# Decode attention on one core: two heads per pass on 64 partitions each, V in 64 KB runs, one loop over all pairs

## Chip, cores, metric

One NeuronCore of one Trainium2 chip; its neighbours are idle. The metric is device time in microseconds for one execution.

## The reference

One new token for 2 batches attends over a key/value cache of 32 heads x 16384 keys x 128 (bf16); beside it runs a small MLP mixer on the same input, and a gate mixes the two. Cut to the part that matters:

```python
B, Sq, D = 2, 1, 1024
H, Sk, Dh = 32, 16384, 128
q = (x @ wq).reshape(B, Sq, H, Dh).transpose(0, 2, 1, 3)
scores = einsum("bhqd,bhkd->bhqk", q, k_cache) * Dh ** -0.5
o = einsum("bhqk,bhkd->bhqd", softmax(scores), v_cache)
a = o.transpose(0, 2, 1, 3).reshape(B, Sq, H * Dh) @ wo
# b = mixer MLP on x (weights w2, w3, w4);  result: g * a + (1 - g) * b
```

K and V are 64 x 4 MB each (a head of one batch: 16384 x 128 x 2 bytes), 537 MB in all, and 33 MB of weights. Each byte is used once.

## The kernel before

It loops over the 64 (head, batch) pairs g. A ring of four slots of 32 KB per partition (4 MB) takes all loads in queue order; a load is issued when a slot is released. A head is spread over all 128 partitions, 128 keys each.

```python
NRS = 4                                   # ring slots, 32 KB per partition each
def kv_src(T, g):
    h, b = g // 2, g % 2
    return T[b, h].rearrange("(p j) d -> p (j d)", p=P)      # 128 partitions x 32 KB
def q_k(g): queue_load(("k", g), [... e.dma_start(ring[:, idx, :], kv_src(A_k, g))])
def q_v(g): queue_load(("v", g), [... e.dma_start(ring[:, idx, :], kv_src(A_v, g))])

def do_T(g, u):      # K, 32x32 blocks transposed in place, an eighth of a slot at a time
    ap = ring[:, slot_of[("k", g)], u * JU * Dh:(u + 1) * JU * Dh].bitcast(F32)
    ev_T[(g, u)] = pl.add("dve", lambda e: e.transpose(ap, ap), waits=(arrived(("k", g)),), sig=True)
# do_S(g, u): 4 score matmuls of 512 columns; after u == NU - 1: release(("k", g), ev)
# softmax chain: do_rmax do_mt do_m do_mb do_negm do_exp do_PT (max, exp, transposed P), do_l do_rc (1/sum)
# do_PV(g): 32 matmuls of 512 columns; then release(("v", g), ev).  do_ext, do_OT: output column

for g in range(G + 2):                    # software pipeline over g, g-1, g-2
    if g < G: do_Z(g)
    for u in range(NU):
        if g < G: do_T(g, u); do_S(g, u)
        if u == 1 and 0 <= g - 2 < G: do_ext(g - 2); do_OT(g - 2)
    if g < G: do_rmax(g); ...; do_exp(g); do_PT(g)
    if 0 <= g - 1 < G: do_PV(g - 1); do_accc(g - 1)
    if g < G: do_l(g); do_rc(g)
GL, GE = 4, G - 2                         # heads 4..61 run in a hardware loop (two per turn); the rest is written out
# ... (cuts: weights, MLP, gate, output projection)
```

The load order is K0, K1, V0, K2, V1, ...; the last loads are pieces of wo, and the last piece's matmuls end the program.

Of the kernel before, what the change touches and what calls it, by code (L numbers as in the profile page):

```python
# [23 lines left out]
class _Plan:  # L24
# [18 lines left out]
    def add(self, eng, fn, waits=(), sig=False):  # L43
        ev = None
        if sig:
            self.cnt[eng] += 1
            ev = _Ev(self.esem[eng], self.cnt[eng])
        self.ops[eng].append((self._merge(waits), fn, ev, 1))
        return ev

    def dma(self, eng, fn, sem, waits=()):
        key = sem.num
        self.dcnt[key] = self.dcnt.get(key, 0) + 16
        ev = _Ev(sem, self.dcnt[key])
        self.ops[eng].append((self._merge(waits), fn, ev, 16))
        return ev
# [10 lines left out]
    @staticmethod  # L67
    def _put(eng, op, waits, base=None, delta=None):
        _, fn, ev, inc = op
        for w in waits:  # L70
            eng.wait_ge(w.sem, w.val if base is None else base * delta[w.sem.num] + w.val)  # L71
        ins = fn(eng)
        if ev is not None:
            ins.then_inc(ev.sem, inc)
# [44 lines left out]
def build_kernel(nc, A_x, A_k, A_v, A_wq, A_wo, B_w1, B_w2, B_w3, B_w4, gate_w, out, dbg=None):  # L119
# [9 lines left out]
    NU = 8  # L129
    JU = J // NU  # L130
    NBP = 4
    G = B * H
    NBD = D // P
# [22 lines left out]
    with ExitStack() as st:  # L156
# [10 lines left out]
        dsel = sb("dsel", [P, 4], BF16)  # L167
# [9 lines left out]
        Z = sb("Z", [P, 2, NBP, ZW], BF16)  # L177
        P_sb = sb("P_sb", [P, 2, NCOL], BF16)
        PT_sb = sb("PT_sb", [P, 2, NCOL], BF16)
        acc_sb = sb("acc_sb", [P, 512], BF16)  # L180
        rowsum = sb("rowsum", [P, 2], F32)
        rmax_bf = sb("rmax_bf", [P, 2], BF16)
        m_sb = sb("m_sb", [1, 2], BF16)
        negm = sb("negm", [P, 2], F32)
        recip = sb("recip", [P, 2], F32)
        OT_sb = sb("OT_sb", [P, G], BF16)
        OTp = sb("OTp", [P, 2], BF16)
        rA = sb("rA", [P, 2], F32)
# [48 lines left out]
        pconst(lambda e: e.memset(ones_f[:, :], 1.0))  # L237
        pconst(lambda e: e.memset(neg_half[:, :], -0.5))
# [8 lines left out]
        e0 = pconst(lambda e: e.memset(dsel[:, :], 0.0))  # L247
        for cg in range(4):
            pconst(aff(dsel[32 * cg:32 * cg + 32, :], -8 * (cg // 2), [[-2, 4]], 1), (e0,))
        e0 = pconst(lambda e: e.memset(rowm[:, :, :], 0.0))  # L250
        ev_rowm = pconst(aff(rowm[:, :, :], 0, [[-32, 4], [-2, NU]], 1), (e0,))
        pconst(lambda e: e.memset(Z[:, :, :, :], 0.0))
# [13 lines left out]
        slot_of = {}  # L266
        slot_free = {i: () for i in range(NRS)}
# [7 lines left out]
        def queue_load(key, fns):  # L275
            dma_q.append((key, fns))

        def pump():
            while dma_q and slot_free:
                key, fns = dma_q.pop(0)  # L280
                idx = next(iter(slot_free))
                waits = slot_free.pop(idx)
                slot_of[key] = idx
                for k, fn in enumerate(fns):
                    dsem = s_ring[idx] if len(fns) == 1 else s_tail[k]
                    dma_done[key] = dma_done[key, k] = pl.dma("sp", (lambda e, fn=fn, idx=idx: fn(e, idx)), dsem,
                                                              waits=waits if k == 0 else ())

        def release(key, ev):
            idx = slot_of[key]  # L290
            assert idx not in slot_free
            slot_free[idx] = tuple(ev) if isinstance(ev, (tuple, list)) else (ev,)
            pump()
# [42 lines left out]

        def q_load(key):
            queue_load(key, wloads[key])

        def kv_src(T, g):  # L340
            h, b = g // 2, g % 2
            return T[b, h].rearrange("(p j) d -> p (j d)", p=P)

        def q_k(g):
            queue_load(("k", g), [lambda e, idx: e.dma_start(ring[:, idx, :], kv_src(A_k, g))])

        def q_v(g):
            queue_load(("v", g), [lambda e, idx: e.dma_start(ring[:, idx, :], kv_src(A_v, g))])
# [37 lines left out]
        def st_gate():  # L386
# [10 lines left out]
                              waits=(e4,), sig=True)  # L397
            e5 = pl.add("dve", lambda e: e.tensor_tensor(gm[:, :], gT[:, 2:4], m2[:, :], op=ALU.mult),
# [153 lines left out]
        q_k(0)  # L552
        for g in range(1, G + 2):
            if g < G:
                q_k(g)
            if g - 1 < G:
                q_v(g - 1)
        for pi in range(len(wo_parts)):
            q_load(("wo", pi))
# [51 lines left out]
        def S_ps(par):  # L611
            return banks[3 + par]

# [3 lines left out]
        l_ps = banks[0][:, 128:129]  # L617
        oT_ps = banks[7][:, 0:1]

        ev_T = {}; ev_Z = {}; ev_S = {}; ev_P = {}; ev_PT = {}; ev_PV = {}; ev_OT = {}; ev_OTc = {}; ev_rmax = {}; ev_m = {}; ev_mt = {}  # L620
        ev_mb = {}; ev_negm = {}; ev_l = {}; ev_rc = {}; ev_accc = {}; ev_ext = {}

        def do_Z(g):
            pg = g % 2
            ev_Z[g] = pl.add("pool", lambda e: e.tensor_tensor(
                Z[:, pg, :, ZO:ZO + P].rearrange("p t (i c) -> p t i c", c=32)[:, :, :, 0],
                q4_f[:, :, g:g + 1].broadcast_to([P, NBP, 4]), mask4[:, :].unsqueeze(1).broadcast_to([P, NBP, 4]), op=ALU.mult),
                waits=(ev_q4, ev_const, ev_S.get(g - 2)), sig=True)

        def do_T(g, u):  # L630
            ap = ring[:, slot_of[("k", g)], u * JU * Dh:(u + 1) * JU * Dh].bitcast(F32)
            ev_T[(g, u)] = pl.add("dve", lambda e: e.transpose(ap, ap), waits=(arrived(("k", g)),), sig=True)  # L632

        def do_S(g, u):
            pg = g % 2
            kv = ring[:, slot_of[("k", g)], u * JU * Dh:(u + 1) * JU * Dh].rearrange("p (j b k t) -> p j b k t", j=JU, b=2, k=32)
            for bp in range(NBP):
                last = bp == NBP - 1
                w = ()
                if bp == 0:  # L640
                    w = (ev_T[(g, u)],)
                    if u == 0:
                        w += (ev_Z[g], ev_P.get(g - 2)) + (pro_ev if g < 2 else ())
                ev = pl.add("pe", lambda e, bp=bp: e.matmul(  # L644
                    S_ps(pg)[:, 0:NCOL], lhsT=Z[:, pg, bp, ZO - 2 * u:ZO - 2 * u + P], rhs=kv[:, :, bp // 2, :, bp % 2],
                    start=(u == 0 and bp == 0), stop=(u == NU - 1 and last), skip_group_check=True),
                    waits=w, sig=(last and u == NU - 1))
            if u == NU - 1:
                ev_S[g] = ev
                release(("k", g), ev)  # L650

        def do_PV(g):
            pg = g % 2
            vv = ring[:, slot_of[("v", g)], :].rearrange("p (u j d) -> p u j d", u=NU, j=JU)
            w = (ev_PT[g], arrived(("v", g)), ev_accc.get(g - 1))
            for jj in range(JU):
                for hf in range(2):
                    cg = 2 * hf + jj % 2
                    last = jj == JU - 1 and hf == 1
                    ev = pl.add("pe", lambda e, jj=jj, hf=hf, cg=cg: e.matmul(  # L660
                        acc_ps[32 * cg:32 * cg + 32, 0:512], lhsT=PT_sb[:, pg, 32 * jj:32 * jj + 32], rhs=vv[:, 4 * hf:4 * hf + 4, jj, :],
                        start=(jj < 2), stop=(jj >= JU - 2), tile_position=(0, 32 * cg), skip_group_check=True), waits=w, sig=last)
                    w = ()
            ev_PV[g] = ev
            release(("v", g), ev)

        def do_rmax(g):
            pg = g % 2
            e1 = pl.add("dve", lambda e: e.tensor_reduce(rA[:, pg:pg + 1], S_ps(pg)[:, 0:NCOL], axis=AX.X, op=ALU.max),  # L669
                        waits=(ev_S[g],), sig=True)  # L670
            ev_rmax[g] = pl.add("dve", lambda e: e.tensor_scalar(rmax_bf[:, pg:pg + 1], rA[:, pg:pg + 1], cAB[:, 1:2], None, op0=ALU.add),  # L671
                                waits=(e1, ev_cab if g == 0 else None, ev_mt.get(g - 2)), sig=True)

        def do_mt(g):
            pg = g % 2
            ev_mt[g] = pl.add("pe", lambda e: e.transpose(mt_ps, rmax_bf[:, pg:pg + 1], ident[:, :]),  # L676
                              waits=(ev_rmax[g], ev_m.get(g - 1), ev_ident if g == 0 else None) + (pro_ev if g == 0 else ()), sig=True)

        def do_m(g):
            pg = g % 2  # L680
            ev_m[g] = pl.add("dve", lambda e: e.tensor_reduce(m_sb[0:1, pg:pg + 1], mt_ps, axis=AX.X, op=ALU.max),  # L681
                             waits=(ev_mt[g], ev_mb.get(g - 2)), sig=True)

        def do_mb(g):
            pg = g % 2
# [171 lines left out]
```

## Time and profile before

| | before |
|---|---|
| time | 1333.47 us (1333.34 to 1333.58, 3 runs) |
| HBM traffic | 570.4 MB |
| rate over the span / from 300 to 1200 us | 429 / 432 GB/s |
| time for two heads (K and V), late in the run | 38.86 us |

The last row is the mean time between two loads into the same ring slot, by their last completions in the trace; in this kernel a slot comes round every fourth 4 MB load.

Abbreviations in the profile: PE is the matrix engine and PEld its weight loads, DVE the vector engine, ACT the scalar engine, POOL GpSimd, SP the engine that issues the loads; q1, q8 are DMA queues; L644 is line 644 of the kernel. "Granted clock" is the share of its full clock that PE was given, "DMA share" the share of time in which the 16 DMA engines were busy.

The main queue's packets fill 99.7% of the span on all 16 engines, while no compute engine is over 65%. A K load is issued 25.2 us and a V load 31.2 us before it lands, though 4 MB take 9.7 us: loads queue behind one another, and the DMA engines never run out of work.

The same by windows, 300 to 1200 us (each engine's busy time, then granted clock, DMA share, GB/s):

```profile
core 0: us, PE busy (x) PEld busy (x) DVE busy (x) ACT busy (x) POOL busy (x), PEclk, DMA share, GB/s
300.00:1200.00 900.00, 600.75 (x3327) 230.22 (x3326) 545.23 (x695) 63.28 (x138) 18.77 (x94) 0.81 1.00 432
```

The DMA share is 1.00 here: in this stretch the time is bytes over rate, and only the rate or the bytes can change it.

### The profile page before, as it was taken

How to read it: one execution, taken by the hardware profiler on the slowest of the kernel's cores; microseconds unless marked ns; L12 is line 12 of the kernel's file. 1: busy time of each engine (PE TensorE's matmuls, PEld its weight loads, DVE VectorE, ACT ScalarE, POOL GpSimd, SP SyncE). 2: the span in 40 equal slices, each digit the busy share in tenths (PEclk: the TensorE clock that was granted, in tenths of full speed). 3: DMA queues.
4: the chain of work that ended last, by engine and by line, in shares of the span. 5: the costliest groups of instructions: out<-in, count | busy, mean ns of one | idle time of the engine just before them, and what ended most of it. 6: DMA issues, size and time to landing. Idle time of an engine off the chain costs nothing.

```text
span 1331.4 us, 14124 instructions
## 1 busy us (share of the span) xinstructions
PE 860.8 (65%) x5466; PEld 343.8 (26%) x5466; DVE 762.6 (57%) x1000; ACT 89.7 (7%) x195; POOL 32.9 (2%) x161
## 2 busy tenths in 40 slices
PE   3466666667666666666766676676667666666765
PEld 3322222222222222222222222222222222222222
DVE  1076566566656656665665666566566656656661
ACT  0000000000000000000000000000000000000000
POOL 1000000000000000000000000000000000000000
PEclk9978887787888778778878878977787788778787
DMA  9999999999999999999999999999999999999998
GB/s 401 431 425 433 433 428 435 428 434 432 432 431 428 437 429 432 432 431 434 428 432 432 432 432 429 433 432 432 431 430 435 430 431 433 432 431 430 433 431 344
DMA packets 21652, 570.65 MB, mean 429 GB/s; under 512 B 2291, under 2 KB 2307, under 8 KB 2694
## 3 DMA queue, kind: packets, MB, share of 16 engines
q1 hardware_dynamic: 21608, 570.44, 99.7%
q8 instruction: 11, 0.18, 0.1%
q14 instruction: 3, 0.02, 0.0%
q10 hardware_dynamic: 30, 0.01, 0.0%
HBM read 570.44 MB, written 0.00 MB: 428 GB/s over the span
## 4 chain that ended last, share of the span: by engine, by line
DMA 64%; PE 25%; DVE 8%; issue 2%; SPq 0%; DVEq 0%; ACT 0%; POOL 0%
DMA ring<-in_A_k_cache_dram 61%; PE ps L644 23%; DVE ring L632 7%; DMA ring<-in_A_wo_dram 2%; DMA ring<-in_A_wq_dram 2%; DVE OTp L727 1%; PE ps L461 0%; PE ps L590 0%; SPq L312 0%; PE ps L711 0%; PE ps L490 0%; PE ps L383 0%; DVEq L71 0%; ACT P_sb L697 0%; POOL mv L424 0%
## 5 line engine op out<-in xcount | busy, mean ns | idle before, releaser
L644 PE MATMUL ps<-ring,Z 128*128 128x512 bf16 x2048 | 655.6, 480 | 326.0 <-DVE ring L632 320.2
L632 DVE STREAM_TRANSPOSE ring<-ring 128x1024 f32<-128x1024 f32 x512 | 591.0, 1212 | 117.3 <-DMA ring<-in_A_k_cache_dram 117.3
L644 PEld LDWEIGHTS ps<-ring,Z 128*128 128x128 bf16 x2048 | 216.6, 114 | 692.5 <-issue 376.3
L660 PE MATMUL ps<-ring,PT_sb 128*32 128x512 bf16 x2048 | 123.7, 384 | 2.3 <-DMA ring<-in_A_v_cache_dram 2.3
L697 ACT ACTIVATE P_sb<-ps,negm 128x512 bf16<-128x512 f32 x64 | 44.0, 688 | 1118.9 <-DVE negm L691 1118.9
L727 DVE TENSOR_SCALAR OTp<-ps,recip,gT 128x1 bf16<-128x1 f32 x64 | 17.9, 280 | 159.9 <-PE ps L711 159.9
L669 DVE TENSOR_REDUCE rA<-ps 128x1 f32<-128x512 f32 x64 | 44.2, 691 | 100.4 <-PE ps L644 100.4
L703 DVE STREAM_TRANSPOSE PT_sb<-P_sb 128x512 bf16<-128x512 bf16 x64 | 45.5, 711 | 54.1 <-ACT P_sb L697 54.1
L660 PEld LDWEIGHTS ps<-ring,PT_sb 128*32 128x32 bf16 x2048 | 49.3, 97 | 45.8 <-issue 3.8
L676 PE MATMUL ps<-ident,rmax_bf 128*1 128x128 bf16 x64 | 13.9, 217 | 66.2 <-DVE rmax_bf L671 66.2
L706 ACT ACTIVATE acc_sb<-ps 128x512 bf16<-128x512 f32 x64 | 38.2, 597 | 53.9 <-PE ps L660 53.9
L730 POOL COPY OT_sb<-OTp 128x1 bf16<-128x1 bf16 x64 | 11.9, 186 | 1204.1 <-DVE OTp L727 1204.1
L676 PEld LDWEIGHTS ps<-ident,rmax_bf 128*1 128x1 bf16 x64 | 5.1, 79 | 97.8 <-DVE rmax_bf L671 97.8
L681 DVE TENSOR_REDUCE m_sb<-ps 1x1 bf16<-1x128 bf16 x64 | 18.0, 281 | 19.7 <-PE ps L676 19.7
L711 PEld LDWEIGHTS ps<-dsel,acc_sb 128*128 128x128 bf16 x256 | 20.4, 118 | 33.7 <-issue 30.0
L691 DVE TENSOR_SCALAR negm<-ps,cAB 128x1 f32<-128x1 f32 x64 | 17.7, 277 | 17.2 <-PE ps L686 17.2
L686 PE MATMUL ps<-m_sb,ones_bf 1*128 1x1 bf16 x64 | 11.0, 172 | 24.0 <-DVE m_sb L681 24.0
L718 PEld LDWEIGHTS ps<-rowsum,ones_f 128*128 128x128 f32 x128 | 19.2, 189 | 28.0 <-issue 26.8
L718 PE MATMUL ps<-rowsum,ones_f 128*128 128x1 f32 x128 | 24.7, 262 | 1.2 <-ACT P_sb L697 1.2
L723 DVE RECIPROCAL recip<-ps 128x1 f32<-128x1 f32 x64 | 10.7, 168 | 19.9 <-PE ps L718 19.9
L590 PE MATMUL ps<-xT_bf,ring 128*128 128x2 bf16 x256 | 7.1, 165 | 17.8 <-DMA ring<-in_A_wq_dram 17.8
L711 PE MATMUL ps<-dsel,acc_sb 128*128 128x1 bf16 x256 | 17.5, 172 | 1.1 <-ACT acc_sb L706 1.1
(91 smaller groups left out, 122.9 us busy)
## 6 DMA issues: line engine op xcount, KB each, us to landing
ring<-in_A_k_cache_dram SPq DMA_DIRECT2D x64, 4096.0 KB, 25.2
ring<-in_A_v_cache_dram SPq DMA_DIRECT2D x64, 4096.0 KB, 31.2
ring<-in_A_wq_dram SPq DMA_DIRECT2D x2, 4096.0 KB, 17.5
ring<-in_B_w_dram SPq DMA_DIRECT2D x2, 3584.0 KB, 32.4
ring<-in_B_w_dram SPq DMA_DIRECT2D x1, 4096.0 KB, 28.3
ring<-in_A_wo_dram SPq DMA_DIRECT2D x1, 4096.0 KB, 32.2
ring<-in_B_w_dram SPq DMA_DIRECT2D x1, 3072.0 KB, 29.0
ring<-in_A_wo_dram SPq DMA_DIRECT2D x3, 1024.0 KB, 21.3
```

The source lines that it names most:

```text
L632: ev_T[(g, u)] = pl.add("dve", lambda e: e.transpose(ap, ap), waits=(arrived(("k", g)),), sig=True)
L644: ev = pl.add("pe", lambda e, bp=bp: e.matmul(S_ps(pg)[:, 0:NCOL], lhsT=Z[:, pg, bp, ZO - 2 * u:ZO - 2 * u + P], rhs=kv[:, :, bp // 2, :, ...
L660: ev = pl.add("pe", lambda e, jj=jj, hf=hf, cg=cg: e.matmul(acc_ps[32 * cg:32 * cg + 32, 0:512], lhsT=PT_sb[:, pg, 32 * jj:32 * jj + 32], ...
L669: e1 = pl.add("dve", lambda e: e.tensor_reduce(rA[:, pg:pg + 1], S_ps(pg)[:, 0:NCOL], axis=AX.X, op=ALU.max), waits=(ev_S[g],), sig=True)
L676: ev_mt[g] = pl.add("pe", lambda e: e.transpose(mt_ps, rmax_bf[:, pg:pg + 1], ident[:, :]), waits=(ev_rmax[g], ev_m.get(g - 1), ev_ident i ...
L681: ev_m[g] = pl.add("dve", lambda e: e.tensor_reduce(m_sb[0:1, pg:pg + 1], mt_ps, axis=AX.X, op=ALU.max), waits=(ev_mt[g], ev_mb.get(g - 2) ...
L697: ev_P[g] = pl.add("act", lambda e: e.activation(P_sb[:, pg, :], S_ps(pg)[:, 0:NCOL], ACT.Exp, bias=negm[:, pg:pg + 1], scale=scale, accum ...
L703: ev_PT[g] = pl.add("dve", lambda e: e.transpose(PT_sb[:, pg, :], P_sb[:, pg, :]), waits=(ev_P[g], ev_PV.get(g - 2)), sig=True)
L706: ev_accc[g] = pl.add("act", lambda e: e.activation(acc_sb[:, :], acc_ps[:, 0:512], ACT.Copy), waits=(ev_PV[g], ev_ext.get(g - 1)), sig=True)
L711: ev = pl.add("pe", lambda e, w=w: e.matmul(oT_ps, lhsT=acc_sb[:, w * P:(w + 1) * P], rhs=dsel[:, w:w + 1], start=(w == 0), stop=(w == 3)) ...
L718: ev_l[g] = pl.add("pe", lambda e: e.matmul(l_ps, lhsT=ones_f[:, :], rhs=rowsum[:, pg:pg + 1], start=True, stop=True), waits=(ev_P[g], ev_ ...
L727: ev_OT[g] = pl.add("dve", lambda e: e.tensor_scalar(OTp[:, pg:pg + 1], oT_ps, recip[:, pg:pg + 1], gT[:, pg:pg + 1], op0=ALU.mult, op1=AL ...
```

## The change

Intent: fewer and longer DMA runs, fewer softmax chains, a program that is one loop. Two heads of a batch share a pass: 64 partitions each, 256 keys per partition, so a partition's row is 64 KB in K and in V. V comes as one 8 MB load with 64 KB runs into two adjacent slots; K comes as two halves of 32 KB per row, so that each half's slot is free early. One softmax chain serves the pair; transposes are twice as long. The three-stage pipeline over heads is gone: each pair runs scores, softmax, PV and output in order, and all 32 pairs are turns of one loop.

```diff
-    NU = 8
-    JU = J // NU
+    HP = 2
+    NU = 16
+    JU = HP * J // NU
+    UH = NU // HP
+    NPR = G // HP
...
-        def kv_src(T, g):
-            h, b = g // 2, g % 2
-            return T[b, h].rearrange("(p j) d -> p (j d)", p=P)
+        w_slots = [0, 1, 2, 3, 0, 1, 2]
+        k_slots = (3, 2)
+        def kv_src(T, n):
+            h, b = n // B * HP, n % B
+            return T[b, h:h + HP].rearrange("h (p j) d -> (h p) (j d)", p=P // HP)
+        def q_k(n):
+            for t in range(2):
+                queue_load(("k", n, t), [lambda e, idx, t=t: e.dma_start(ring[:, idx, :], kv_src(A_k, n)[:, t * SLOT:(t + 1) * SLOT])],
+                           (k_slots[t],))
+        def q_v(n):
+            queue_load(("v", n), [lambda e, idx: e.dma_start(ring[:, idx:idx + 2, :].rearrange("p s m -> p (s m)"), kv_src(A_v, n))],
+                       (0, 1))
...
+        TC = 2
+        def do_T(n, c):
+            key, o = ("k", n, c * TC // UH), c * TC % UH * JU * Dh
+            ap = ring[:, slot_of[key], o:o + TC * JU * Dh].bitcast(F32)
+            return pl.add("dve", lambda e: e.transpose(ap, ap), waits=(arrived(key),), sig=True)
...
-        for g in range(G + 2):
-            ... (as above)
+        for n in range(NPR):
+            ev_z = do_Z(n)
+            for c in range(NU // TC):
+                ev_t = do_T(n, c)
+                for t in range(TC):
+                    do_S(n, c * TC + t, ...)
+            ev_pt, ev_rc = do_softmax(n)
+            ev_OT = do_out(n, do_PV(n, ev_pt), ev_rc)
...
-        GL, GE = 4, G - 2
-            first = pl.mark[GL][name]
-            return first, pl.mark[GL + 2][name] - first, (GE - GL) // 2
+            first = pl.mark[0][name]
+            return first, pl.mark[1][name] - first, NPR
```

## The prediction

> **What bounds the kernel now.** The DMA engines. On the page the main DMA queue's packets fill 99.7% of the 16 engines' span. By windows, 300 to 1200 us moves 432 GB/s at DMA share 1.00, while PE is busy 601, DVE 545 and ACT 63 of those 900 us. The chain that ended last gives DMA 64%; its PE and DVE shares only lie between a K landing and the next K issue. By the issue list a K load lands 25.2 us after its issue, V 31.2, against about 9.7 us of transfer (4 MB at 432 GB/s): one or two whole loads always wait behind the one in flight. The Trainium skill ("DMA: Bandwidth & Descriptors", Where 436 GB/s comes from) gives a port ceiling of 435.2 GB/s; this trace is within 1% of it. 570 MB at that ceiling still take 1310 us, so over 2% faster (below 1307) is practically excluded.
>
> **What the change does.**
> - Bytes: unchanged.
> - V: 4096 descriptors of 64 KB instead of 8192 of 32 KB. Packet records before: 8 KB 0.312, 28 KB 1.062, 32 KB 1.218 us. A line through the first two leaves about 12 ns per packet that doesn't grow with size. 256 packets fewer per engine x 12 ns = 3 us, on the critical path, the only such item. If the run is cut in two below the program, zero.
> - 32 DMAs fewer: completion records of 9 ns x 32 per engine = 0.3 us.
> - K: the same 32 KB packets, now half of a 64 KB row. I expect 1.22 us still.
> - Off the path: one softmax chain per pair instead of two; transposes of 2048 instead of 1024 elements (1212 ns now, estimate for double 2.3 us: about 30 us of DVE in all). Score and V matmuls stay 2048 each. DVE and ACT fall; the time doesn't follow.
> - Lost: overlap. Each pair runs scores, softmax, PV, output strictly in order. From the first K half's landing at 0: scores done at 12 us (transposes 9.3, last 8 matmuls 2.4), slot free; second half lands at 9.7, free at 22; softmax to 27; V (8 MB) lands at 29, its slots free by 33 to 35. By then the queue holds K of the next pair until 48.6: V is issued some 14 us ahead of need, K some 17. No bubble.
> - Start: same weight order; the second K half waits for the last w4 matmuls (66.2 us) while the first is in flight until 73. Tail: unchanged, the last wo piece.
>
> **Predicted: 1330 us, range 1322 to 1338.** Chances: faster by over 2% 0.01, within 2% 0.95, slower 0.04.
>
> **What would show the steps right.** DMA share 1.00 in the middle at 433 to 434 GB/s; V packets of 65,536 B at about 2.42 us; K packets at 1.22 us; K issue to landing about 27 us, V about 35; DVE down by roughly 50 us, ACT roughly halved, PE about the same; the chain still led by DMA.
>
> **What would make it wrong.** (1) DMA share below 1 between pairs, a slot freed too late: each 1 us per pair costs 32 us. (2) K packets slowed by the 64 KB row pitch; the skill's row-pitch entry (same page, Latency and other measured facts) starts at 512 KiB, no run here shows 64 KB. (3) 64 KB runs cut in two: 1333. (4) The 16 engines ending differently in the tail (a load's sixteen completions are 3.2 us apart now): +-2 us.

(The 1310 us in it is an estimate from that page's ceiling; at the measured 432 GB/s the same bytes take 1320 us.)

## More of the kernel before

From the page of the kernel before: busy time of each engine, DMA queues (packets, MB, share of the 16 engines' span), the chain that ended last, the two largest groups (busy us, mean ns of one, then idle time and its releaser), and for the K and V loads the KB of each and the median us from issue to landing.

```profile
span 1331.4 us, 14124 instructions
...
PE 860.8 (65%) x5466; PEld 343.8 (26%) x5466; DVE 762.6 (57%) x1000; ACT 89.7 (7%) x195; POOL 32.9 (2%) x161
...
q1 hardware_dynamic: 21608, 570.44, 99.7%
q8 instruction: 11, 0.18, 0.1%
...
DMA 64%; PE 25%; DVE 8%; issue 2%; SPq 0%; DVEq 0%; ACT 0%; POOL 0%
...
L644 PE MATMUL ps<-ring,Z 128*128 128x512 bf16 x2048 | 655.6, 480 | 326.0 <-DVE ring L632 320.2
L632 DVE STREAM_TRANSPOSE ring<-ring 128x1024 f32<-128x1024 f32 x512 | 591.0, 1212 | 117.3 <-DMA ring<-in_A_k_cache_dram 117.3
...
ring<-in_A_k_cache_dram SPq DMA_DIRECT2D x64, 4096.0 KB, 25.2
ring<-in_A_v_cache_dram SPq DMA_DIRECT2D x64, 4096.0 KB, 31.2
```

## The result, and the profile after

| | before | after |
|---|---|---|
| time | 1333.40 us (1333.33 to 1333.58, 4 runs) | 1329.43 us (1329.39 to 1329.61, 4 runs) |
| two heads, late in the run | 38.86 us | 38.78 us |
| last load's sixteen completions, first to last | 3.19 us | 1.88 us |

The ratio is 0.997, 95% interval 0.9953 to 0.9988: small, and clear of noise. Ratios here are the mean time of one kernel's runs over that of the other's runs of the same rounds, so not quite the ratio of the medians in the table. Executions over 1.5% slower than the fastest of the same kernel are left out of the means.

The page after, the lines that answer to those of before:

```profile
span 1327.6 us, 12590 instructions
...
PE 803.9 (61%) x5306; PEld 327.0 (25%) x5306; DVE 659.3 (50%) x521; ACT 45.7 (3%) x99; POOL 20.1 (2%) x101
...
q1 hardware_dynamic: 17000, 570.43, 99.7%
q8 instruction: 8, 0.13, 0.0%
...
DMA 72%; DVE 16%; PE 6%; issue 6%; SPq 0%; ACT 0%
...
L664 PE MATMUL ps<-ring,Z 128*128 128x512 bf16 x2048 | 540.0, 418 | 217.8 <-DVE ring L657 217.3
L657 DVE STREAM_TRANSPOSE ring<-ring 128x2048 f32<-128x2048 f32 x256 | 569.0, 2280 | 108.6 <-DMA ring<-in_A_k_cache_dram 108.6
...
ring<-in_A_k_cache_dram SPq DMA_DIRECT2D x64, 4096.0 KB, 27.8
```

The V loads' line stands in the list of DMA issues of the kernel after:

```profile
ring<-in_A_v_cache_dram SPq DMA_DIRECT2D x32, 33.0
```

And its windows, 300 to 1200 us:

```profile
300.00:1200.00 900.00, 553.53 (x3233) 216.05 (x3225) 469.67 (x347) 32.21 (x70) 8.81 (x46) 0.79 1.00 433
```

DVE lost 103 us of busy time, ACT half of its own, PE 57 us, and the time fell by 4. The DMA queue is as full as before (99.7%, share 1.00); its rate went from 432 to 433 GB/s. K and V still land 28 and 33 us after their issue, so loads still queue. There are 4.6 thousand packets fewer, and 8 instruction packets in place of 11.

The packet records of the two traces, by size (count, mean us of one):

```
size       before            after
 28 KB      256  1.070        256  1.069
 32 KB    16640  1.218       8448  1.218
 64 KB        -              4096  2.422
```

So a 64 KB run is one packet of 65,536 bytes. A K packet still takes 1.218 us although it is now half of a 64 KB row.

Where do the 4.0 us come from? Time per two heads fell by 0.076 us, which is 2.4 us over 32 pairs. The rest, about 1.5 us, does not accumulate in the steady part. The trace has the completion of each of the 16 engines for each load, and shows it there: before, the spread from the first to the last engine was 1.81 us for the load that landed at 180.1 us and 3.09 us for the next, at 191.1, and it stayed near 3.2 to the end; after, it is 1.9 from 56 us to the end. The last load shows both parts: its first completion came at 1324.98 us before and at 1322.53 after, 2.45 us earlier; its last at 1328.17 and 1324.41, 3.76 us earlier. (The two profiled executions took 1333.23 and 1329.41 us, 3.82 apart, so what the medians show beyond 3.8 lies between executions.) A load counts as landed only when its last engine is done, so the slower of two equally busy kernels can be the one whose slowest engine is further behind. (The Trainium skill, "DMA: Bandwidth & Descriptors", Why a DMA increments its semaphore by 16 and not by 1, says that the engines finish independently and only the full count means that all data landed. This trace agrees: each load has sixteen completions, the last load's 3.19 us apart before and 1.88 after.)

What set one engine back at 180 us? These records lie there, in the kernel before (start us, queue, kind, bytes, duration):

```
180.58 q8 instruction       16384 B  1.086 us
181.65 q1 hardware_dynamic  32768 B  1.694 us      (1.218 usual)
```

An instruction fetch of 16 KB took a DMA engine for 1.09 us, and a data packet that starts at its end took 0.48 us more than usual: 1.56 us together. That both ran on the same engine is read from their times; the trace does not say which engine a packet ran on. It was the ninth fetch of that run. Other fetches show the same: in a_peel24 (below) each of the 27 fetches among the K and V loads has one such packet, 0.46 to 0.55 us longer than usual.

That leaves two theories for the gain, and a rival:

- **P, packets:** each long run saves the fixed cost of one packet. Worth 2.4 us.
- **F, fetches:** the one-loop program is shorter, needs fewer instruction fetches, and its slowest DMA engine is hit once in place of twice. Worth about 1.3 us.
- **C, compute or number of DMAs:** half the softmax chains, longer transposes, 32 loads fewer. By the trace worth nothing.

### The profile page after: what moved, and what is told of

The parts are those of the page before. It is cut to its first block, busy times and chain, and to the rows that moved or that the text cites. A ratio compares the mean times of both kernels' runs of the same rounds, so it can differ in the third digit from the quotient of the medians.

```text
span 1327.6 us, 12590 instructions
## 1 busy us (share of the span) xinstructions
PE 803.9 (61%) x5306; PEld 327.0 (25%) x5306; DVE 659.3 (50%) x521; ACT 45.7 (3%) x99; POOL 20.1 (2%) x101
## 3 DMA queue, kind: packets, MB, share of 16 engines
q1 hardware_dynamic: 17000, 570.43, 99.7%
## 4 chain that ended last, share of the span: by engine, by line
DMA 72%; DVE 16%; PE 6%; issue 6%; SPq 0%; ACT 0%
DMA ring<-in_A_k_cache_dram 66%; DVE ring L657 16%; PE ps L664 5%; DMA ring<-in_B_w_dram 2%; DMA ring<-in_A_wo_dram 2%; DMA ring<-in_A_wq_dram 2%; SPq L324 0%; PE ps L514 0%; PE ps L612 0%; PE ps L485 0%; PE ps L405 0%; DVE orow L756 0%; DVE q_f L624 0%; PE ps L734 0%; PE ps L621 0%
## 5 line engine op out<-in xcount | busy, mean ns | idle before, releaser
L664 PE MATMUL ps<-ring,Z 128*128 128x512 bf16 x2048 | 540.0, 418 | 217.8 <-DVE ring L657 217.3
L657 DVE STREAM_TRANSPOSE ring<-ring 128x2048 f32<-128x2048 f32 x256 | 569.0, 2280 | 108.6 <-DMA ring<-in_A_k_cache_dram 108.6
L700 PE MATMUL ps<-ring,PT_sb 128*32 128x512 bf16 x2048 | 183.4, 537 | 152.7 <-DMA ring<-in_A_v_cache_dram 152.7
L700 PEld LDWEIGHTS ps<-ring,PT_sb 128*32 128x32 bf16 x2048 | 67.6, 130 | 255.4 <-DMA ring<-in_A_v_cache_dram 155.4
L674 DVE TENSOR_REDUCE rA<-ps 128x1 f32<-128x512 f32 x32 | 22.1, 691 | 64.3 <-PE ps L664 64.3
L685 ACT ACTIVATE P_sb<-ps,negm 128x512 bf16<-128x512 f32 x32 | 22.0, 687 | 851.5 <-DVE negm L683 851.5
L689 PE MATMUL ps<-rowsum,hsel 128*128 128x1 f32 x128 | 23.8, 290 | 37.9 <-ACT P_sb L685 37.9
L687 DVE STREAM_TRANSPOSE PT_sb<-P_sb 128x512 bf16<-128x512 bf16 x32 | 22.8, 711 | 27.0 <-ACT P_sb L685 27.0
L709 ACT ACTIVATE acc_sb<-ps 128x512 bf16<-128x512 f32 x32 | 19.1, 597 | 363.4 <-PE ps L700 363.4
L689 PEld LDWEIGHTS ps<-rowsum,hsel 128*128 128x128 f32 x128 | 21.1, 234 | 40.7 <-ACT P_sb L685 40.7
## 6 DMA issues: line engine op xcount, KB each, us to landing
ring<-in_A_k_cache_dram SPq DMA_DIRECT2D x64, 4096.0 KB, 27.8
```

The lines of the kernel that those rows point to most:

```text
L657: return pl.add("dve", lambda e: e.transpose(ap, ap), waits=(arrived(key),), sig=True)
L664: ev = pl.add("pe", lambda e, bp=bp: e.matmul(S_ps[:, 0:NCOL], lhsT=Z[:, bp, ZO - 2 * u:ZO - 2 * u + P], rhs=kv[:, :, bp // 2, :, bp % 2], ...
L674: e1 = pl.add("dve", lambda e: e.tensor_reduce(rA[:, :], S_ps[:, 0:NCOL], axis=AX.X, op=ALU.max), waits=(ev_S[n],), sig=True)
L685: e7 = pl.add("act", lambda e: e.activation(P_sb[:, :], S_ps[:, 0:NCOL], ACT.Exp, bias=negm[:, 0:1], scale=scale, accum_out=rowsum[:, 0:1] ...
L687: e8 = pl.add("dve", lambda e: e.transpose(PT_sb[:, :], P_sb[:, :]), waits=(e7,), sig=True)
L689: e9 = pl.add("pe", lambda e, hp=hp: e.matmul(l_ps[:, hp:hp + 1], lhsT=hsel[:, hp, :], rhs=rowsum[:, 0:1], start=True, stop=True, skip_gro ...
```

## The experiments

Labels: a_ is the kernel after with one thing changed; c_ goes further. All gave correct results. "Pair" is the time of two heads in the steady part, "fetches" the q8 packets of the run, "spread" the time from the first to the last engine's completion of the last wo load. The experiments were run in two batches on two chips; the kernel before took 1333.50 and 1333.39 us in them, so times of different rows compare within some 0.1 us.

| run | time us | ratio to before (95%) | pair us | fetches | spread us |
|---|---|---|---|---|---|
| before | 1333.40 | | 38.856 | 11 | 3.19 |
| after | 1329.43 | 0.997 (0.9953 to 0.9988) | 38.780 | 8 | 1.88 |
| a_v32 | 1332.04 | 0.9989 (0.9975 to 1.0003) | 38.858 | 8 | 2.11 |
| a_peel8 | 1331.01 | 0.9982 (0.9968 to 0.9996) | 38.78, to 760 us | 16 | 3.63 |
| a_peel24 | 1335.45 | 1.0014 (1.0001 to 1.0028) | 38.79, between jumps | 34 | 8.10 |
| a_soft2 | 1329.46 | 0.9971 (0.9956 to 0.9986) | 38.777 | 8 | 1.64 |
| a_soft4 | 1468.9 | 1.1016 (1.0996 to 1.1037) | 43.2 | 8 | 0.64 |
| a_kone | 1425.55 | 1.069 (1.0671 to 1.071) | 41.55 | 8 | 1.63 |
| c_k64 | 1328.35 | 0.9962 (0.9949 to 0.9976) | 38.702 | 9 | 3.04 |
| c_k64s | 1327.13 | 0.9954 (0.994 to 0.9967) | 38.702 | 8 | 2.02 |

### a_v32: V in 32 KB runs again, all else kept

```diff
-        k_slots = (3, 2)
+        k_slots = (3, 1)
-            ... e.dma_start(ring[:, idx:idx + 2, :].rearrange("p s m -> p (s m)"), kv_src(A_v, n))], (0, 1))
+            ... e.dma_start(ring[:, 0:3:2, :], kv_src(A_v, n).rearrange("q (s m) -> q s m", s=2))], (0, 2))
```
(The weights' slots 1 and 2 swap too, and the PV matmuls read the two slots. Still one DMA of 8 MB.)

> The kernel after, with one thing undone: V is still one load of 8 MB per pair, but into two ring slots that don't touch, so each partition's 64 KB arrive as two runs of 32 KB. Theory P (the gain in the steady part is the fixed cost per packet): no 65,536 B packets left, time per pair back from 38.78 to 38.86 us, so 32 x 0.076 = 2.4 us more, 1331.8 us. Rival F (what counts is how far the slowest of the 16 DMA engines has been set back by instruction fetches): same program length, so no change, 1329.4. Rival C (fewer DMAs, one softmax chain per pair): all kept, 1329.4.

1332.04 us, 2.6 more than after. The trace has 16640 packets of 32 KB and none of 64 KB, and the pair takes 38.858 us, as in the kernel before. The window says the same:

```profile
300.00:1200.00 900.00, 554.61 (x3241) 216.35 (x3232) 467.51 (x346) 32.22 (x70) 8.81 (x46) 0.79 1.00 432
```

All of the steady gain hangs on the run length: back to 432 GB/s with the same compute, the same number of DMAs and the same program. P holds. Against the kernel before, which has the same pair time, it is still 1.4 us faster (the ratio's interval just includes 1, but no run of the one lies within the range of the other); its spread at the end is 2.11 us, not 3.19. The first completion of its last load comes at 1325.00 us, as before (1324.98). That remainder is what F has to explain.

### a_peel8 and a_peel24: a longer program, the same work

```diff
-            return first, pl.mark[1][name] - first, NPR
+            return first, pl.mark[1][name] - first, NPR - 8        # a_peel24: NPR - 24
```
(and the output column's index as a constant in the pairs that are written out)

> The kernel after with the first 8 of 32 pairs written out before the loop: same work, same loads, a longer program. Theory F (each 16 KB instruction fetch holds one DMA engine for about 1.1 us and costs it about 1.5 with the packet behind it; the fetches go round over the engines, 7 before the last loads now, so each engine is hit at most once; the slowest engine sets every landing): some 4 or 5 fetches more, an engine hit twice, the sixteen completions of a load 3.1 us apart instead of 1.9, and the end 1.2 to 1.5 us later: 1330.7 us. Time per pair late in the run unchanged at 38.78. Theory P alone: 1329.4.

The note is wrong in one point: this edit loops over the first 24 pairs and writes out the last 8. That made the test cleaner. The time was 1331.01 us, 1.6 more than after. There were 8 fetches more and not 4 or 5, one for each pair written out. Time per pair was 38.78 up to 760 us, as expected. Up to 1072 us the spread stayed between 1.9 and 2.3; the load after that, at 1083, had 3.23, and nine fetches had started by then. At the end it was 3.63.

> The kernel after with the last 24 of 32 pairs written out behind a loop of 8 (the run before this of that kind also wrote out the last 8, not the first 8 as its note said). Same loads and work. Theory F: one 16 KB instruction fetch per pair, so some 32 in place of 8; they go round over eight of the sixteen DMA engines, so the slowest one is hit four times in place of once, 1.5 us each: completions of a load some 6.4 us apart at the end (1.9 now), the time 4.5 us longer, about 1334 us, slower than the kernel before the change. Theory P alone: 1329.4.

1335.45 us: the kernel after, with nothing changed but the number of copies of its loop body, is now slower than the kernel before. There were 34 fetches, two more than expected:

```profile
q1 hardware_dynamic: 17000, 570.43, 99.3%
q8 instruction: 34, 0.56, 0.2%
```

The spread of a load's sixteen completions, at the four loads where it jumps, with the fetches that had started before that load was through:

```
a_peel24   load landed at   462.7 us   2.15 -> 3.59 us    9 fetches
           load landed at   745.6 us   3.69 -> 5.31 us   17 fetches
           load landed at  1037.8 us   5.18 -> 6.64 us   25 fetches
           load landed at  1320.7 us   6.70 -> 8.17 us   33 fetches
a_peel8    load landed at  1082.8 us   2.01 -> 3.23 us    9 fetches
before     load landed at   191.1 us   1.81 -> 3.09 us    9 fetches
```

In these three runs, apart from the first fetch, which opened the spread by 1.2 to 1.5 us, the slowest engine falls back at the 9th, 17th, 25th and 33rd fetch; at no other does the spread grow by more than 0.35. So the fetches go round over eight engines, and the first of them to be hit again sets the pace. The trace does not name the engines, but a load's sixteen completion times tell them apart. In a_peel24 each fetch from the 9th to the 13th puts one of these times back by 1.4 to 1.6 us and leaves the other fifteen within 0.1 us of where they were. At the end of that run seven engines lie within 0.8 us of the first to finish (itself included), six 5.8 to 6.1 us behind, two 8.1: 34 fetches are four rounds of eight and two more. At the end of a_peel8, after 16 fetches, seven lie within 0.9 us and eight 3.2 to 3.6 us behind. (The sixteenth engine, at 3.9 and 2.2 us, fits no q8 round; by the times, its steps follow 8 KB instruction packets of another queue, q14.) The time was expected at about 1334 because the fifth round was not foreseen; 1.5 us for one more round is the difference.

F holds, and its size too: 6.2 us of spread more than after, 6.0 us of time more. The first completion of the last load hardly moved (1322.53 us after, 1322.40 in a_peel8, 1322.61 in a_peel24), so the longer program cost nothing else.

### c_k64 and c_k64s: K in 64 KB runs as well

With four slots, an 8 MB K load has no room until the last scores are done. A fifth slot and alternating halves give it room: K of even pairs lies in slots 1 and 2, of odd pairs in 0 and 1, and each pair works off slot 1 first, which is the one that the next K shares.

```diff
-    NRS = 4
+    NRS = 5
-            for t in range(2):
-                queue_load(("k", n, t), [lambda e, idx, t=t: e.dma_start(ring[:, idx, :], kv_src(A_k, n)[:, t * SLOT:(t + 1) * SLOT])], ...
+            queue_load(("k", n), [lambda e, idx: e.dma_start(ring[:, idx:idx + 2, :].rearrange("p s m -> p (s m)"), kv_src(A_k, n))],
+                       ((1, 2), (0, 1))[n % 2])
-                release(key, ev)
+                release_slot(slot_of[key] + u // UH, ev)
-            return first, pl.mark[1][name] - first, NPR
+            return first, pl.mark[2][name] - first, NPR // 2
```
(V in slots 3 and 4; halves in the order slot 1 first.)

> The kernel after, with K too in runs of 64 KB: one 8 MB load per pair, a fifth ring slot, and alternate order of the two halves so that the next K's two slots are free by half time. Theory P: K packets of 65,536 B, each saving the same 8 ns against two of 32 KB that the V packets save, time per pair 38.71 us, 2.2 us less in all, about 1327.2 us; if the longer loop body of two pairs brings one instruction fetch more onto an engine that already had one, 1.3 us of it are lost again (1328.5). Rival C (number of DMAs or softmax work): 32 DMAs fewer of 9 ns per engine, 0.3 us, 1329.1.

All 8192 cache packets are of 65,536 bytes, and the pair takes 38.702 us, 0.078 less than after and the same step as from 32 to 64 KB in V (0.078 us over 8 packets per engine: 10 ns a packet, where the note had 8). The window reads

```profile
300.00:1200.00 900.00, 539.73 (x3266) 219.52 (x3265) 465.11 (x347) 32.23 (x70) 8.87 (x46) 0.78 1.00 434
```

But the time is 1328.35 us, only 1.1 us better than after: the loop body of two pairs costs one more fetch, and the ninth came at 1321.1 us. The spread was 1.66 for the load that landed at 1321.2 and 3.04 for the last one. That is the lost 1.3 us of the expectation.

> K and V both in 64 KB runs, and in addition 96 matmuls of the prologue left out that multiply weights by an all-zero vector (w2 is still loaded), to shorten TensorE's program by about 12 KB. Theory F: eight fetches in place of nine, no engine is hit twice before the last load, the spread at the end falls from 3.0 to about 1.8 us and the time by 1.2 us to about 1327.1 us. If the ninth fetch had no part in the end time: 1328.3, as without the shortening.

```diff
-    put(mlp_chain(key, halves, 0, NBD, NBD, hs_ps, lambda kc: shT_bf[:, kc, :], "const", "hs", D, last=False)
-            + [row_stage(key, list(range(NBD)), 0, NBD, lambda kc: shT_bf[:, kc, :], "const", last=True)], key)
+        put([w2_unused], key)       # hs stays zero; the slot is released once w2 has arrived
```

1327.13 us with 8 fetches and a spread of 2.02 us: the step of 1.2 us came as expected, from leaving out 96 matmuls that were nowhere near the critical path (for one token the mixer's shifted vector is all zeros, so they added nothing; w2 is still loaded). The edit also frees w2's ring slot earlier, but that is not what helped: the last load's first completion came only 0.17 us earlier than in c_k64 (1320.04 against 1320.21), its last one 1.18 us earlier. This is the fastest version here, 2.3 us below after and 6.3 below before.

### a_soft2 and a_soft4: is the halved softmax part of the gain?

```diff
-            ev_pt, ev_rc = do_softmax(n)
+            for _ in range(2):                                      # a_soft4: range(4)
+                ev_pt, ev_rc = do_softmax(n, ev_pt if _ else ev_S[n])
```

> The kernel after with the softmax chain of each pair done twice, one after the other (same result): 3.7 us more in the serial chain of each pair, back to as many chains as before the change. The serial chain of a pair is now 30.7 us (from the first transpose to the output column, without its waits for K and V) in a period of 38.8, so 34.4 still fit: 1329.4 us, within 0.5. If the halved softmax work were part of the gain: up to 32 x 3.7 = 118 us more.

1329.46 us against 1329.43. Twice the softmax chains cost nothing; the pair time is 38.777. Of C, the chains are out. (The two other parts of C were kept in a_v32, and it lost the steady gain; so they do not carry it either.)

> The same with the softmax chain done four times: 11.1 us more per pair, 41.8 us of serial chain in a period of 38.8. If slack is what hides the chain, it now runs out: 3 us per pair longer, about 1425 us (1390 to 1460), DMA share below 1. If the queue's lead of 14 us (V issued 13 us before the K loads ahead of it are through) were the measure of the slack: 1329.4.

1468.9 us: slack does run out, but the estimate was 44 us short and its range too low. Timeline of a_soft4, one pair (start us, duration us, engine, line, operation; L700 is PV, L657 the K transposes):

```profile
613.14 0.69 DVE L674 TENSOR_REDUCE rA<-ps 128x1 f32<-128x512 f32 x1 [2.01 <-PE ps L664]
...
629.18 0.14 PEld L700 LDWEIGHTS ps<-ring,PT_sb 128*32 128x32 bf16 x8
629.18 6.00 PE L700 MATMUL ps<-ring,PT_sb 128*32 128x512 bf16 x64
...
635.23 0.33 SPq L369 DMA_DIRECT2D ring<-in_A_v_cache_dram  x1
...
636.40 0.22 DVE L713 SCALAR_TENSOR_TENSOR OT_sb<-ps,gTt,recip 128x2 f32 x1 [6.94 <-PE ps L711]
636.88 17.66 DVE L657 STREAM_TRANSPOSE ring<-ring 128x2048 f32<-128x2048 f32 x8 [0.26 <-issue]
...
656.55 0.69 DVE L674 TENSOR_REDUCE rA<-ps 128x1 f32<-128x512 f32 x1 [2.01 <-PE ps L664]
```

From the first reduction at 613.14 to PV at 629.18 are 16.0 us; the first chain takes 3.7, the repeats about 4.1, because the next one waits behind the reciprocal of the row sum before it. PV takes 6.0, output and the first transpose's start 1.7, scores 19.7. The sum is 43.4, the measured pair 43.2: each pair is now one serial chain, and the next K transposes start at 636.88 without a wait for DMA. In the kernel after the same sum is about 31 in 38.8. So the slack of the strict order is about 8 us per pair, and not the 14 us by which V is issued ahead.

### a_kone: K in one 8 MB load with four slots

```diff
-            for t in range(2): queue_load(("k", n, t), ..., (k_slots[t],))
+            queue_load(("k", n), [... e.dma_start(ring[:, idx:idx + 2, :].rearrange("p s m -> p (s m)"), kv_src(A_k, n))], (2, 3))
-                release(key, ev)
+                if u == NU - 1:
+                    release(key, ev)
```

> The kernel after with one 8 MB K load per pair and still four ring slots: the next K can only be issued when the last scores of this K are done. K at 0: transposes 17.8 us, last matmuls 2.2, free at 20; V is through 19.4 us after K. So the queue runs dry in each pair, by some 0.7 us plus the start of a load (about 1.6 us, as at the start of the program): 2.3 us x 32 = 75 us more, about 1404 us (1385 to 1430), with DMA share near 0.94. If only packets counted and slot timing did not: 1327.

1425.55 us, within the range, above the estimate. Timeline of a_kone, one pair:

```profile
607.32 0.33 SPq L364 DMA_DIRECT2D ring<-in_A_k_cache_dram  x1
...
617.38 0.33 SPq L367 DMA_DIRECT2D ring<-in_A_v_cache_dram  x1
...
629.19 17.66 DVE L655 STREAM_TRANSPOSE ring<-ring 128x2048 f32<-128x2048 f32 x8 [10.43 <-DMA ring<-in_A_k_cache_dram]
```

The K load is issued at 607.32 and lands at 629.19: 21.9 us, though 8 MB take 19.35 in c_k64. In the kernel after a 4 MB K load is issued 27.8 us before it lands. The queue runs dry once per pair (here no packet is under way from 648.17 us, the end of V, to 649.81, the first of the next K), and starting it again costs 2.5 us where 1.6 had been taken from the start of the program. The pair is 41.55 us, 2.85 more than c_k64's; the rest of the difference lies at the start, where the first K lands at 88.3 us and not at 82.9, and at the end. The page shows the DMA share:

```profile
q1 hardware_dynamic: 12392, 570.43, 94.3%
```

Longer runs alone are worth 0.08 us per pair; the slot timing that the change kept by halving K is worth 2.85.

## Why the prediction was right

The time was predicted at 1330, measured 1329.43.

- **"The DMA engines" bound the kernel.** Right: twice the softmax chains changed nothing (a_soft2), and the run length alone moved the steady part (a_v32, c_k64).
- **V packets "3 us" and 32 DMAs fewer "0.3 us".** The mechanism was right, the sum of 3.3 too large by 0.9: the steady part gave 2.4. A saved packet is worth 10 ns on its engine (a_v32 against after: 0.078 us per pair over 8 packets per engine); the line through two other packet sizes had given 12. The 32 DMAs show no gain at all: a_v32, with three loads per pair, takes 38.858 us, and before, with four, 38.856. The packets took 2.42 us as predicted, the rate was 433 GB/s.
- **K unchanged at 1.22 us in a 64 KB pitch.** Right: 1.218.
- **No bubble, slots free in time.** Right for the outcome: share 1.00, K 27.8 us from issue to landing (27 predicted), V 33.0 (35). The slack was given as "some 14 us"; that is V's lead in the queue. The margin against more work in the chain is about 8 us (a_soft4).
- **DVE "down by roughly 50 us", PE "about the same".** Off: DVE fell by 103, PE by 57. The transposes gave 22 of DVE's; the rest is the halved chain, for which 50 less the 30 of the transposes had left only some 20. None of it is on the path, so the time did not notice.
- **The engines' ends in the tail, "+-2 us".** The item was listed, as luck without a sign. It is not luck: the loop over all pairs shortens the program below nine instruction fetches before the end. It gave 1.3 us, a third of the gain. With 2.4 from packets that makes 3.7 of 4.0; the last 0.3 us is mostly a difference between executions, as the two profiled ones are 3.8 apart. The two misses, 0.9 us too much for packets and nothing for fetches, partly cancelled: that the prediction came within 0.6 us is in part luck.

Not shown: the kernel before with fewer than nine fetches was not run; as it is written, its pipeline and rotating ring let only heads 4 to 61 be a loop. F's share in before against after rests on the jump at its ninth fetch and on the two peeled kernels.

## What to carry to other kernels

When the DMA share is 1.00 and the rate within 1% of the ports' ceiling, as here, less compute work buys nothing; what is left are fixed costs per packet, so make the runs long, but only if the slots still come free before the queue is through. When every load waits for its slowest engine, look at the spread of a load's completions and at the instruction queue: a program that is a tight loop can beat the same work written out. Measure the slack of a serial chain by lengthening it, not by how early its loads are issued.

## What the Trainium skill lacked or had wrong

- "DMA: Bandwidth & Descriptors" (Queues, rings and completion order) says that an engine takes turns between its queues. "Runtime: NRT & Kernel Launch" (Instruction fetch mechanics) says that programs are fetched by DMA in 16 KiB blocks and calls the cost of crossing a block mostly hidden. No page tells that these fetches take DMA engines away from data: here 16 KB each, 1.09 us, and 0.48 us more for the data packet behind. The slowest engine fell back by 1.2 to 1.6 us at the 9th, 17th, 25th and 33rd fetch; 34 fetches in place of 8 cost 6.0 us of 1329.
- "DMA: Bandwidth & Descriptors" (Where 436 GB/s comes from) gives 435.2 GB/s as ceiling and says that for HBM to SBUF an HBM side of about 358 binds, while its own table measures 425 and a note below that table gives 358 as a core's part only when both cores of a pair stream. One core alone sustained 432 GB/s with 32 KB runs and 434 with 64 KB runs over 900 us here; the port ceiling was the one to reckon with.
- The same page (Why small descriptors are slow) names a fixed cost per packet and treats it as a matter of short descriptors. It is still there at 32 KB: 10 ns per packet and engine, 0.2% of the time per 4096 packets saved.
- The same page (Anatomy of one DMA) gives a fixed cost of about 2.0 us per DMA, fitted for loads issued from GpSimd; no page gives it for a load from the sync queue that meets an empty queue in mid-run. Here 8 MB took 21.9 us from issue to landing against 19.35 in a full queue, 2.5 us more.
